# A cached-attention and MLP kernel for one token: K's first loads move to the head of the DMA stream, and two rows of wq share a load behind them

## The chip, the cores and the metric

The kernel runs on one core of a Trainium2 chip. The metric is device time in microseconds (us), the median of several runs. A profile of one more execution shows what each engine did. The engines are TensorE (PE in the profile; PEld for its weight loads), VectorE (DVE), ScalarE (ACT), GpSimd (POOL) and SyncE (SP). Loads from memory are issued by SyncE's and ScalarE's sequencers and carried out by sixteen DMA engines.

## What is computed

One token x of 1024 values is normalized and goes through two branches, whose results are added to x. Branch A is attention of 32 query heads over a cache of 4 key/value heads, of which the last 4096 positions are used. Branch B normalizes once more and applies a two-layer MLP. Cut to what matters, with B = Sq = 1, D = 1024, Hq = 32, Hkv = 4, Dh = 128, W = 4096, F = 3584, all in bf16:

```python
xn = layernorm(x)
q = (xn @ wq).reshape(1, 1, 32, 128)
k = repeat(k_cache[:, :, Sk - 4096:, :], 8, axis=1)
v = repeat(v_cache[:, :, Sk - 4096:, :], 8, axis=1)
o = softmax(q k^T * 128 ** -0.5) @ v
a = o.reshape(1, 1, 4096) @ wo
b = gelu(layernorm(xn) @ w1 + b1) @ w2 + b2
out = x + a + b
```

Nearly all bytes are read once: K and V 4 MB each, `wq` and `wo` 8 MB each, `w1` and `w2` 7 MB each.

## The kernel before

Four buffers of 4 MB (`slot[0]` to `slot[3]`, 128 partitions by 32 KB each) take all large loads in turn. `slot[0]` receives K, `slot[1]` and `slot[2]` receive `wq` rows 0 to 3 and 4 to 7 of each partition, and `slot[3]` is scratch for K's transposes. Later `w1`, V, `w2` and `wo` go into the same buffers as these come free.

Each of K's four head groups is one load (`load_k`, L193): 32 rows of 32 KB, each row going to one partition, group g to partitions g, g + 4, g + 8 and so on (L194). `wq` is seen as 128 partitions of eight rows of 8 KB (L190).

Six loads are issued ahead of everything else, at L199: by SyncE row 0 of `wq` and K's groups 0 to 3, and by ScalarE the small x (32 rows of 64 bytes). Then comes a barrier of all engines (L203), and after it the work that the class `Plan` (L15) writes out: the code lists operations with the names that each reads and writes, in the order in which each engine is to run them, and `Plan.emit` (L27) adds the waits between engines. Nothing is reordered. Lines 235 to 238 enter the early loads into this list without issuing them again, so that later operations can wait for their semaphores. Lines 244 to 246 issue the rest of `wq`: row 1, rows 2 and 3, rows 4 to 7.

SyncE's queue is served in the order of issue. After `wq` it issues the small `b1` and `b2` (L322, L323), the two halves of `w1` (L383, L384), V (L387), three parts of `w2` (L431, L432) and seven parts of `wo` (L506, L509), each once the buffer it overwrites is free. The line in the profile for all these is that of the helper that issues, L213.

What the other engines do around the change:

- GpSimd builds constants from L254 on, of which `spread` (L255) is needed by the first matmul.
- TensorE spreads x over the partitions (four small matmuls, L277), sums for the first LayerNorm, and then runs the product with `wq` in three pieces: a loop over rows 0 and 1 (L369), rows 2 and 3 (L370 to L377), and a loop over rows 4 to 7 (L378). Matmuls without a loop carry the helpers' lines L227 and L233, and weight loads L219.
- VectorE runs the LayerNorm's small operations (L280 to L313). Then it transposes K in four pieces of 128 x 4096 values (L334), each of which waits for all four groups of K. From L343 it copies ten of sixteen blocks of the result into `kT`; ScalarE copies the other six (L339). Scores, softmax, the product with V, and sums over 21 rows of `w2` (L482) follow.
- At the end TensorE takes `wo` rows as they land (L227). VectorE adds the bulk into `run[0]` (L550), the result is cast (L569, L570), and SyncE and ScalarE store one half each (L572, L573).

Of the kernel before, what the change touches and what calls it, by code (L numbers as in the profile page):

```python
# [132 lines left out]
def kernel(  # L133
# [14 lines left out]
    nc = tc.nc  # L148
    P = 128
    D = A_x.shape[-1]  # L150
    Hkv = A_k_cache.shape[1]
    Sk = A_k_cache.shape[2]
    Dh = A_k_cache.shape[3]
    NQ = A_wq.shape[1]
    Hq = NQ // Dh
    REP = Hq // Hkv
    Fd = B_w1.shape[1]
    W = min(4096, max(256, Sk // 4))
# [15 lines left out]
    def sb(name, shape, dt):  # L174
        return nc.alloc_sbuf_tensor(name, shape, dt).ap()

    def ps(name, shape):
        return nc.alloc_psum_tensor(name, shape, FP32).ap()

    slot = [sb(f"slot{i}", [P, 16384], BF16) for i in range(4)]  # L180
    kT = sb("kT", [P, 4, 4, W // 4], BF16)
    acc2 = ps("acc2", [P, 2, 512])
# [3 lines left out]

    x_flat = A_x.rearrange("a b d -> (a b d)")
    k_sb, kt_scr = slot[0], slot[3]
    k_sem = [nc.alloc_semaphore(f"k{g}") for g in range(Hkv)]
    wq_v = A_wq.rearrange("(p c) n -> p c n", p=P)  # L190
    wq_sem = nc.alloc_semaphore("wq0")

    def load_k(g):  # L193
        return nc.sync.dma_start(out=k_sb[g:P - Hkv + g + 1:Hkv, :],  # L194
                                 in_=A_k_cache[0, g, Sk - W:Sk, :].rearrange("(r c) d -> r (c d)", r=P // Hkv))

    x32 = sb("x32", [Hq, Hq], BF16)
    x_sem = nc.alloc_semaphore("x32")
    for i, sem in [(nc.sync.dma_start(out=slot[1][:, 0:NQ], in_=wq_v[:, 0, :]), wq_sem)] + [(load_k(g), k_sem[g]) for g in range(Hkv)] + [(nc.scalar.dma_start(out=x32, in_=x_flat.rearrange("(a j) -> a j", a=Hq)), x_sem)]:  # L199
        i.then_inc(sem, 16)  # L200
        tc.no_tile_sem_insts.add(i.ins.name)
    tc.close()
# [2 lines left out]
    plan = Plan(nc)  # L205
    pe, dve, act, pool, sp = nc.tensor, nc.vector, nc.scalar, nc.gpsimd, nc.sync

    def op(eng, fn, r=(), w=()):
        plan.add(eng, fn, r, w)
# [5 lines left out]
    def ldw(w_ap, pos, r):  # L215
        def go():
            with nc.discard():
                i = pe.ldweights(w_ap, tile_position=pos).ins
            return pe.add_instruction(mybir.InstLdweights(  # L219
                name=nc.get_next_instruction_name(), engine=i.engine, tile_size=(P, 32), tile_position=pos, ins=i.ins, outs=i.outs))  # L220
        op("pe", go, r, ())

    def mm(out_ap, w_ap, x_ap, start, stop, pos, r, w):
        def go():
            with nc.discard():
                i = pe.matmul(out_ap, lhsT=w_ap, rhs=x_ap, start=start, stop=stop, tile_position=pos).ins
            return pe.add_instruction(mybir.InstMatmult(  # L227
                name=nc.get_next_instruction_name(), engine=i.engine, start_tensor_calc=start, stop_tensor_calc=stop,
                tile_size=i.tile_size, tile_position=i.tile_position, ins=i.ins, outs=i.outs, ldweights=False))
        op("pe", go, r, w)  # L230

    def mm32(out_ap, w_ap, x_ap, start, stop, r, w, pos=None):
        op("pe", lambda: pe.matmul(out_ap, lhsT=w_ap, rhs=x_ap, start=start, stop=stop, tile_position=pos), r, w)  # L233

    plan.add("sp", lambda: None, (), ("wq0",), wq_sem)
    for g in range(Hkv):
        plan.add("sp", lambda: None, (), (f"k{g}",), k_sem[g])
    plan.add("act", lambda: None, (), ("x32",), x_sem)

    w1_v = B_w1.rearrange("(p c) n -> p c n", p=P)  # L240
    w2_v = B_w2.rearrange("(p c) n -> p c n", p=P)
    wo_v = A_wo.rearrange("(p c) n -> p c n", p=P)
    wq_t = [slot[1 + i].rearrange("p (r n) -> p r n", r=4) for i in range(2)]
    wq_cuts = ((0, 1, 2), (0, 2, 4), (1, 0, 4))
    for i, a, b in wq_cuts:
        dma("sp", wq_t[i][:, a:b, :], wq_v[:, 4 * i + a:4 * i + b, :], (), (f"wq{4 * i + a}",))

# [48 lines left out]
    xw = sb("xw", [P, 96 + C * P], BF16)  # L296
# [32 lines left out]
    scr = kt_scr.rearrange("p (s f) -> p s f", s=NS)  # L329
    k2 = k_sb.rearrange("p (s f) -> p s f", s=NS)  # L330
    T5 = kt_scr.rearrange("p (s c a j) -> p s c a j", s=NS, a=4, j=32)
    T3 = kt_scr.rearrange("p (c a j) -> p c a j", a=4, j=32)
    for s in range(NS):
        op("dve", lambda s=s: dve.transpose(out=scr[:, s, :], in_=k2[:, s, :]), ("k0", "k1", "k2", "k3", "slot0"), (f"scr{s}",))  # L334
    pairs = [(R, Cd) for R in range(4) for Cd in range(4)]
    ACT_PAIRS = 6
    for s0, s1 in ((0, 1), (1, 2), (2, 4)):
        for (R, Cd) in pairs[:ACT_PAIRS]:
            op("act", lambda s0=s0, s1=s1, R=R, Cd=Cd: act.copy(out=kT[32 * Cd:32 * Cd + 32, R, s0:s1, :].rearrange("p s (c j) -> p (s c) j", j=32),  # L339
                                                                in_=T3[32 * R:32 * R + 32, 32 * s0:32 * s1, Cd, :]), [f"scr{s}" for s in range(s0, s1)], (f"kTa{R}{Cd}{s0}",))  # L340
    kt_keys = [f"kTa{R}{Cd}{s}" for (R, Cd) in pairs[:ACT_PAIRS] for s in range(3)]
    for n, (R, Cd) in enumerate(pairs[ACT_PAIRS:]):
        op("dve", lambda R=R, Cd=Cd: dve.tensor_copy(out=kT[32 * Cd:32 * Cd + 32, R, :, :].rearrange("p s (c j) -> p (s c) j", j=32),  # L343
                                                     in_=T3[32 * R:32 * R + 32, :, Cd, :]), [f"scr{s}" for s in range(NS)], (f"kTd{R}{Cd}",))
# [8 lines left out]
    def pe_loop(name, steps, body):  # L353
        at = pe.alloc_register(f"{name}_at")
        pe.reg_mov(at, 0)
        pe.br(f"{name}_rows")
        only = [mybir.EngineType.PE]
        nc.enter_bb(f"{name}_rows", valid_engines=only)
        body(pe.snap(at, min_val=0, max_val=steps - 1))
        pe.reg_add(at, at, 1)  # L360
        pe.br_lt(at, steps, f"{name}_rows", f"{name}_done")
        nc.enter_bb(f"{name}_done", valid_engines=only)

    def wq_rows(i, per):
        def rows(at):
            for u in range(per):
                n = per * at + u
                for b in range(2):
                    pe.matmul(acc2[:, b, :], lhsT=xw[:, bass.ds(32 * n + 512 * i, P)],  # L369
                              rhs=slot[1 + i][:, bass.ds(1024 * n + 512 * b, 512)], start=False, stop=False)  # L370
        return rows

    qz, zrow = qm.rearrange("p g h -> p (g h)")[0:Hq, :], spread.rearrange("p u n -> p (u n)")
    for b in range(2):
        mm32(acc2[:, b, :], qz, zrow, True, False, ("qm", "spread"), ("acc2",))
    op("pe", lambda: pe_loop("wq0", 8, wq_rows(0, 1)), ("xw", "wq0", "wq1"), ("acc2",))
    for c in (2, 3):  # L377
        for t in range(4):  # L378
            ldw(xw[:, 96 + P * c:97 + P * c], (0, 32 * t), ("xw",))
        for b in range(2):  # L380
            for t in range(4):
                j = 2 * (3 - t) + b
                mm(acc2[32 * t:32 * t + 1, b, :], xw[:, 96 + P * c:97 + P * c], wq_t[0][:, c, j * 512:(j + 1) * 512],  # L383
                   False, False, (0, 32 * t), ("wq0", "wq1", "wq2", "slot1"), ("acc2",))  # L384
    op("pe", lambda: pe_loop("wq1", 8, wq_rows(1, 2)), ("xw", "wq4", "slot2"), ("acc2",))
    for b in range(2):
        mm32(acc2[:, b, :], qz, zrow, False, True, ("qm", "spread", "slot2"), ("acc2",))  # L387
# [21 lines left out]
    for b in range(2):  # L409
        for hh in range(4):  # L410
            k = 4 * b + hh
# [130 lines left out]
    def wo_row(c):  # L542
        i, r = divmod(c, 16)
        return wo_t[i][:, r, :], f"wo0{r // 8 * 8}" if i == 0 else f"wo1{max(a for a in cuts if a <= r)}"
# [9 lines left out]
    for c in range(NB, CWO):  # L554
        wap, key = wo_row(c)
# [49 lines left out]
```

## Time and profile before

| what | value |
|---|---|
| median of 3 runs | 100.47 us (100.42 to 100.51) |
| the profiled execution | 100.62 us, of which the span is 98.8 us |
| granted TensorE clock, mean | 0.896 |
| busy: TensorE / VectorE / ScalarE / GpSimd | 57.2 / 73.9 / 30.7 / 10.0 us |
| bytes read | 39.86 MB, 403 GB/s over the span |
| K, one group: time from issue to landing (median of four) | 9.8 us |
| x: time from issue to landing | 3.5 us |
| last wq load (4 MB): time from issue to landing | 27.0 us |

The span runs from the first to the last instruction of the execution that was profiled; the rest of its time lies before and after. The strip of slices shows the busy share of each engine in tenths, in 40 equal stretches of the span. In a line of the waits, the numbers are the idle time in total, how often it happened and the longest; in a line of the timeline or of the chain, the start and the duration. A line of the windows gives the stretch, its length, the busy time and number of instructions of PE, PEld, DVE, ACT and POOL, then the granted clock, the DMA share and GB/s, where a packet counts in the window in which it starts. The trace also records every packet of the DMA engines by itself: its start, its duration, its size and its queue, but not which of the sixteen engines carried it.

### The profile page before, as it was taken

Reading aid. Unit: us, or ns where it says so; the run is one execution under the profiler, and the core shown is the slowest. Engines: PE = TensorE matmul, PEld = TensorE weight load, DVE = VectorE, ACT = ScalarE, POOL = GpSimd, SP = SyncE. Lnnn points to the kernel's source line nnn. Section 1 sums busy time; section 2 is a strip of 40 time slices with the busy share of each in tenths; the row PEclk is TensorE's granted clock in tenths of the full one; section 3 lists DMA queues with packets and bytes.
Section 4 is the critical chain, followed back from the end, with each engine's and each line's share of the span. In section 5 each row is a group of like instructions: output and inputs, shape, how many; then the busy total and the mean of one; then the engine's idle time right before and its main releaser. Section 6 shows DMA issues by size and latency. Waiting matters only on the chain.

```text
span 98.8 us, 961 instructions
## 1 busy us (share of the span) xinstructions
PE 57.2 (58%) x323; PEld 16.2 (16%) x220; DVE 73.9 (75%) x75; ACT 30.7 (31%) x29; POOL 10.0 (10%) x22
## 2 busy tenths in 40 slices
PE   0032040598200699960899586667670999594792
PEld 0022000123000233410202121212210111110130
DVE  0023776999999999999102677899999999999431
ACT  0050000089999899992001075100000000000001
POOL 0072580000000680000000000000000000000000
PEclk9999999999985556997558999999999589999999
DMA  3999979999999999999799999999998999999970
GB/s 50 448 418 451 464 328 458 441 511 438 424 424 405 395 453 453 395 441 464 338 424 424 418 441 413 463 424 429 487 418 383 431 431 424 424 424 405 405 265 1
DMA packets 3132, 39.86 MB, mean 403 GB/s; under 512 B 438, under 2 KB 444, under 8 KB 828
## 3 DMA queue, kind: packets, MB, share of 16 engines
q1 hardware_dynamic: 3082, 39.86, 95.4%
q10 hardware_dynamic: 50, 0.00, 0.0%
HBM read 39.86 MB, written 0.00 MB: 403 GB/s over the span
## 4 chain that ended last, share of the span: by engine, by line
DVE 36%; DMA 32%; PE 20%; issue 5%; SPq 2%; ACT 2%; DVEq 0%
DMA slot<-in_A_wo_dram 20%; DVE slot L334 18%; DVE kT L343 13%; DMA slot<-in_A_k_cache_dram 13%; PE qo_ps L495 10%; PE sc_ps L227 6%; PE acc L227 2%; SPq L194 2%; ACT e L450 1%; DVE eTb L454 1%; DVE m_loc L435 1%; PE acc L233 1%; DVE q_sb L388 1%; ACT sc L427 1%; DVE res L569 0%
## 5 line engine op out<-in xcount | busy, mean ns | idle before, releaser
L339 ACT COPY kT<-slot 32x1024 bf16<-32x1024 bf16 (+1 forms) x18 | 23.9, 1327 | 14.3 <-DVE slot L334 14.1
L482 DVE SCALAR_TENSOR_TENSOR run<-slot,hTf,run 128x1024 f32<-128x1024 bf16 x20 | 24.2, 1272 | 0.0
L369 PE MATMUL acc<-slot,xw 128*128 x48 | 15.7, 494 | 12.6 <-DMA slot<-in_A_wq_dram 12.2
L334 DVE STREAM_TRANSPOSE slot<-slot 128x4096 bf16<-128x4096 bf16 x4 | 17.4, 4414 | 1.2 <-DMA slot<-in_A_k_cache_dram 1.2
L343 DVE COPY kT<-slot 32x4096 bf16<-32x4096 bf16 x10 | 13.2, 1316 | 0.2
L495 PE MATMUL qo_ps<-slot,eTb 128*128 (+1 forms) x32 | 10.2, 382 | 5.1 <-issue 4.0
L227 PE MATMUL sc_ps<-slot,o 128*1 128x512 bf16 x48 | 9.1, 378 | 2.8 <-DMA slot<-in_A_wo_dram 2.8
L369 PEld LDWEIGHTS acc<-slot,xw 128*128 x48 | 5.5, 115 | 23.5 <-issue 21.1
L570 ACT CAST res<-acc 33x224 bf16<-33x224 f32 x1 | 0.3, 338 | 20.1 <-PE acc L227 20.1
L227 PE MATMUL sc_ps<-kT,qm 128*32 128x512 bf16 x32 | 6.1, 973 | 0.3 <-DVE qm L416 0.3
L495 PEld LDWEIGHTS qo_ps<-slot,eTb 128*128 (+1 forms) x32 | 3.1, 96 | 12.0 <-issue 8.7
L428 DVE COPY sc<-sc_ps 128x512 f32<-128x512 f32 x1 | 0.7, 691 | 5.7 <-PE sc_ps L227 5.7
L227 PE MATMUL sc_ps<-slot,hT 128*1 128x512 bf16 x14 | 4.7, 509 | 0.1
L538 ACT CAST o<-misc 128x32 bf16<-128x32 f32 x1 | 0.2, 186 | 14.6 <-PE misc L233 14.6
L219 PEld LDWEIGHTS <-o 128*1 128x1 bf16 x40 | 2.4, 83 | 12.4 <-issue 11.8
L233 PE MATMUL misc<-x,spread 32*128 32x8 bf16 x4 | 0.3, 168 | 6.2 <-POOL spread L255 6.2
L249 DVE MEMSET mhalf<- 128x1 f32 x1 | 0.1, 59 | 5.0 <-PEq L203 5.0
L233 PE MATMUL acc<-spread,qm 32*128 32x512 bf16 x4 | 1.6, 498 | 3.7 <-POOL qm L315 3.7
L227 PE MATMUL acc<-slot,yT 128*1 128x448 bf16 x64 | 3.4, 353 | 0.0
L427 ACT COPY sc<-sc_ps 128x512 f32<-128x512 f32 x1 | 0.6, 585 | 8.8 <-PE sc_ps L227 8.8
L251 ACT ACT_TABLE_LOAD x1 | 1.3, 1283 | 4.8 <-PEq L203 4.8
L227 PE MATMUL acc<-slot,o 128*1 128x288 bf16 (+1 forms) x32 | 2.2, 272 | 0.6 <-DMA slot<-in_A_wo_dram 0.6
(88 smaller groups left out, 46.0 us busy)
## 6 DMA issues: line engine op xcount, KB each, us to landing
slot<-in_B_w_dram SPq DMA_DIRECT2D x3, 3584.0 KB, 16.6
slot<-in_A_wo_dram SPq DMA_DIRECT2D x3, 2048.0 KB, 22.8
slot<-in_A_k_cache_dram SPq DMA_DIRECT2D x4, 1024.0 KB, 9.8
slot<-in_A_wq_dram SPq DMA_DIRECT2D x1, 4096.0 KB, 27.0
slot<-in_A_v_cache_dram SPq DMA_DIRECT2D x1, 4096.0 KB, 16.1
slot<-in_A_wq_dram SPq DMA_DIRECT2D x2, 1024.0 KB, 9.2
slot<-in_A_wq_dram SPq DMA_DIRECT2D x1, 2048.0 KB, 17.8
slot<-in_B_w_dram SPq DMA_DIRECT2D x1, 2048.0 KB, 21.5
```

Source lines behind the costliest of these rows:

```text
L194: return nc.sync.dma_start(out=k_sb[g:P - Hkv + g + 1:Hkv, :], in_=A_k_cache[0, g, Sk - W:Sk, :].rearrange("(r c) d -> r (c d)", r=P // Hkv))
L219: return pe.add_instruction(mybir.InstLdweights(name=nc.get_next_instruction_name(), engine=i.engine, tile_size=(P, 32), tile_position=pos ...
L227: return pe.add_instruction(mybir.InstMatmult(name=nc.get_next_instruction_name(), engine=i.engine, start_tensor_calc=start, stop_tensor_c ...
L233: op("pe", lambda: pe.matmul(out_ap, lhsT=w_ap, rhs=x_ap, start=start, stop=stop, tile_position=pos), r, w)
L251: op("act", lambda: act.activation(out=dummy[:, 0:1], in_=mhalf[0:1, 0:1], func=ACT.Exp), ("mhalf",), ("act_warm",))
L334: op("dve", lambda s=s: dve.transpose(out=scr[:, s, :], in_=k2[:, s, :]), ("k0", "k1", "k2", "k3", "slot0"), (f"scr{s}",))
L339: op("act", lambda s0=s0, s1=s1, R=R, Cd=Cd: act.copy(out=kT[32 * Cd:32 * Cd + 32, R, s0:s1, :].rearrange("p s (c j) -> p (s c) j", j=32), ...
L343: op("dve", lambda R=R, Cd=Cd: dve.tensor_copy(out=kT[32 * Cd:32 * Cd + 32, R, :, :].rearrange("p s (c j) -> p (s c) j", j=32), in_=T3[32 ...
L369: pe.matmul(acc2[:, b, :], lhsT=xw[:, bass.ds(32 * n + 512 * i, P)], rhs=slot[1 + i][:, bass.ds(1024 * n + 512 * b, 512)], start=False, st ...
L427: op("act", lambda: act.copy(out=sc[:, 512:1024], in_=sc_ps[:, 1, :]), ("sc1",), ("scs1",))
L482: op("dve", lambda: dve.scalar_tensor_tensor(out=t, in0=wap, scalar=hTf[:, c:c + 1], in1=t, op0=ALU.mult, op1=ALU.add), (key, "hTf", f"run ...
L495: return pe.matmul(qo_ps, lhsT=cols, rhs=v4[:, :, c, :], start=first, stop=last)
```

## The change

K moves to the head of SyncE's stream. Its group 0 is split into two loads of sixteen rows, the even ones and the odd ones (partitions 0, 8, 16 and so on, and 4, 12, 20 and so on). Groups 1 to 3 stay loads of 32 rows. `wq` row 0 leaves the head, and one load issued after the barrier brings rows 0 and 1. The number of SyncE's loads is the same, five ahead of the barrier and three of `wq` behind it. The transposes wait for five semaphores of K instead of four, and the matmuls with `wq` rows 0 to 3 wait for one load less. Every other instruction keeps its place on its engine.

```diff
     k_sb, kt_scr = slot[0], slot[3]
-    k_sem = [nc.alloc_semaphore(f"k{g}") for g in range(Hkv)]
+    RK = P // Hkv
+    k_parts = [(0, 0, 2), (0, 1, 2)] + [(g, 0, 1) for g in range(1, Hkv)]
+    k_sem = [nc.alloc_semaphore(f"k{g}{b}") for g, b, _ in k_parts]
     wq_v = A_wq.rearrange("(p c) n -> p c n", p=P)
-    wq_sem = nc.alloc_semaphore("wq0")
-
-    def load_k(g):
-        return nc.sync.dma_start(out=k_sb[g:P - Hkv + g + 1:Hkv, :],
-                                 in_=A_k_cache[0, g, Sk - W:Sk, :].rearrange("(r c) d -> r (c d)", r=P // Hkv))
+
+    def load_k(g, b, step):
+        rows = A_k_cache[0, g, Sk - W:Sk, :].rearrange("(r c) d -> r (c d)", r=RK)
+        return nc.sync.dma_start(out=k_sb[g + Hkv * b:P - Hkv * (step - b) + g + 1:Hkv * step, :], in_=rows[b:RK - step + b + 1:step, :])
...
-    for i, sem in [(nc.sync.dma_start(out=slot[1][:, 0:NQ], in_=wq_v[:, 0, :]), wq_sem)] + [(load_k(g), k_sem[g]) for g in range(Hkv)] + [(nc.scalar.dma_start(out=x32, in_=x_flat.rearrange("(a j) -> a j", a=Hq)), x_sem)]:
+    for i, sem in [(load_k(*p), s) for p, s in zip(k_parts, k_sem)] + [(nc.scalar.dma_start(out=x32, in_=x_flat.rearrange("(a j) -> a j", a=Hq)), x_sem)]:
...
-    plan.add("sp", lambda: None, (), ("wq0",), wq_sem)
-    for g in range(Hkv):
-        plan.add("sp", lambda: None, (), (f"k{g}",), k_sem[g])
+    k_keys = tuple(f"k{g}{b}" for g, b, _ in k_parts)
+    for key, sem in zip(k_keys, k_sem):
+        plan.add("sp", lambda: None, (), (key,), sem)
...
-    wq_cuts = ((0, 1, 2), (0, 2, 4), (1, 0, 4))
+    wq_cuts = ((0, 0, 2), (0, 2, 4), (1, 0, 4))
...
-        op("dve", lambda s=s: dve.transpose(out=scr[:, s, :], in_=k2[:, s, :]), ("k0", "k1", "k2", "k3", "slot0"), (f"scr{s}",))
+        op("dve", lambda s=s: dve.transpose(out=scr[:, s, :], in_=k2[:, s, :]), k_keys + ("slot0",), (f"scr{s}",))
...
-    op("pe", lambda: pe_loop("wq0", 8, wq_rows(0, 1)), ("xw", "wq0", "wq1"), ("acc2",))
+    op("pe", lambda: pe_loop("wq0", 8, wq_rows(0, 1)), ("xw", "wq0"), ("acc2",))
...
-                   False, False, (0, 32 * t), ("wq0", "wq1", "wq2", "slot1"), ("acc2",))
+                   False, False, (0, 32 * t), ("wq0", "wq2", "slot1"), ("acc2",))
```

## Prediction

> **What bounds the kernel now.** I read the page's strip of slices and its queue table first, then the waits, the chain of waits, the order of SyncE's issues, and last the first microseconds cut into short windows.
>
> ```profile
> span 98.8 us, 961 instructions
> ...
> DMA  3999979999999999999799999999998999999970
> ...
> q1 hardware_dynamic: 3082, 39.86, 95.4%
> ```
>
> SyncE's queue (q1) carries 39.86 MB, and its packets fill 95.4% of sixteen DMA engines' time over the whole span. The strip shows no slice in which the engines stand still between the first and the last. The waits say the same at the end of the kernel:
>
> ```profile
> PE sc_ps L227 <- DMA slot<-in_A_wo_dram: 2.8, 3, 1.3
> ...
> DVE run L550 <- PE sc_ps L227: 1.5, 1, 1.5
> ...
> DVE slot L334 <- DMA slot<-in_A_k_cache_dram: 1.2, 1, 1.2
> ```
>
> TensorE waits for pieces of `wo` to land, VectorE's last sum (L550) waits 1.5 us for TensorE, and VectorE's first transpose of K (L334) waits 1.2 us for K. The third line is where K's arrival is felt. The chain of waits has K in it as well:
>
> ```profile
> 3.10 12.46 DMA slot<-in_A_k_cache_dram
> ...
> 15.58 17.44 DVE slot L334 x4
> ...
> 74.51 19.40 DMA slot<-in_A_wo_dram
> ```
>
> This chain must be read with care. The last line is a load of 1 MB that needed 19.40 us because it was queued behind loads issued earlier. A chain that issues it sooner does not make it land sooner, so the K part of the chain does not bound the end. To see how far it is from bounding, I compare each issue on SyncE with the landing of the load before it (issue time plus time to landing):
>
> ```profile
> 25.46 7.90 SPq L213 DMA_DIRECT2D slot<-in_B_w_dram  x2
> 43.57 0.38 SPq L213 DMA_DIRECT2D slot<-in_A_v_cache_dram  x1
> 46.35 9.38 SPq L213 DMA_DIRECT2D slot<-in_B_w_dram  x3
> 58.77 17.59 SPq L213 DMA_DIRECT2D slot<-in_A_wo_dram  x7
> ```
>
> The load issued at 25.46 stands behind the last `wq` load, which lands at 32.6 (issued 5.61, 27.0 us to landing). The `v` load issued at 43.57 stands behind a `w1` load issued at 33.04 that lands at 49.7 (16.6 us). The smallest margin is that one, 6.1 us. So every issue may move several microseconds either way and the engines still never run out of work. The end is the start of the stream, plus its bytes at the engines' pace, plus a short tail (last piece of `wo` landed at 96.5, last matmul over at 96.83, casts, store).
>
> **The change part by part.** The new order of SyncE's loads is K's group 0 as sixteen rows and sixteen rows, groups 1 to 3, then `wq` rows 0-1, 2-3, 4-7. It was eight loads and is eight loads, with the same bytes. TensorE, VectorE, ScalarE and GpSimd keep every instruction in its place.
>
> *K lands earlier.* It loses the 1 MB in front of it: eight packets of 8 KB on each engine, start to start 0.306 us by the trace's records of single packets, 2.45 us. It landed at 15.56, so now near 13.1. VectorE can't use all of that. Before L334 stand the LayerNorm operations (the last ends at 14.41), and these wait for x.
>
> *x lands later.* x goes through ScalarE's queue, and in the packet records its two rows and its semaphore each come after one packet of the other queue, so three packets pass first. Those were 8 KB (0.309 us); they become K rows of 32 KB (1.213 us each): 3 x 0.904 = 2.7 us later, 4.28 becomes about 7.0. TensorE's first matmul ran at 6.20, held by GpSimd's `spread`, so 1.9 us of this lies under GpSimd and 0.8 us is left. LayerNorm then ends at 15.2 and the transposes start at 15.2 instead of 15.58. Behind that VectorE is earlier by 0.4 us, with 1.5 us of idle before L550 as before. For the end this is worth 0.00. If x came later than that, VectorE would hold the end once LayerNorm ends 2.6 us late (1.18 us of idle before L334 and 1.46 before L550), which needs x at 8.8.
>
> *`wq` rows 0-1 as one load.* TensorE's first loop waited for both rows already. They end at the same place in the stream (6.3 MB in, landing 18.0), so its start stays. Packets of 16 KB take 0.613 us against 2 x 0.309; start to start that saves 2 ns, 8 packets per engine: -0.02 us. `wq` rows 0-1 stop being SyncE's two issues and become one, K's group 0 becomes two: no issue more or less.
>
> *One more cut in K.* Between two loads each engine handles one 4-byte semaphore packet of 9 ns; one is added in K and one goes from `wq`: 0.00. [...]
>
> *The head of the stream.* This is the part with a price. These windows give the DMA share and GB/s in the last two columns:
>
> ```profile
> 0.00:1.75 1.75, 0.00 (x0) 0.00 (x0) 0.00 (x0) 0.00 (x0) 0.20 (x4) 1.00 0.00 0
> 1.75:2.25 0.50, 0.00 (x0) 0.00 (x0) 0.00 (x0) 0.00 (x0) 0.00 (x0) 1.00 1.45 229
> 2.25:2.75 0.50, 0.00 (x0) 0.00 (x0) 0.00 (x0) 0.00 (x0) 0.00 (x0) 1.00 0.44 115
> 2.75:3.25 0.50, 0.00 (x0) 0.00 (x0) 0.00 (x0) 0.00 (x0) 0.00 (x0) 1.00 0.80 314
> 3.25:4.75 1.50, 0.00 (x0) 0.00 (x0) 0.00 (x0) 0.00 (x0) 0.00 (x0) 1.00 1.04 437
> ```
>
> The first load is issued at 0.80 and nothing moves until 1.81. Then for 1.5 us the mean is 219 GB/s, against 437 right after: 1.5 x (1 - 219/437) = 0.75 us of stream time lost. The packet records show how: the sixteen engines start one after another from 1.81 to 2.58 (mean 2.04), and most first packets take 0.55 to 1.24 us instead of 0.31. The first load has 128 rows, eight per engine. The new first load has sixteen rows, one per engine.
>
> The trace of before has no such load at the head, so I bound it. The nearest row for a load of few rows is the last store: issued at 97.38, its packet moves at 98.17, 0.79 us later, against 1.01 for the first of the 128-row load and 1.78 for its last engine. With 0.79 to 1.01 all engines start between 1.59 and 1.81, middle 1.70, which is 0.34 us before the present mean of 2.04. Best case: the whole loss of 0.75 us goes. Worst case: a K load takes longer to issue (0.53 to 0.61 us, against 0.40 for the `wq` load), which starts everything 0.13 to 0.21 us later with no gain. I take the middle value of 0.34, since one descriptor per engine is nearest to the store, and I leave the slowness of the first packets as it is.
>
> The sum: -0.34 - 0.02 = -0.36 us. The profiled execution had a span of 98.8 and 100.62 in all, so 1.8 us lies around the span; it becomes 98.4 and 100.26. The median of the runs is 0.15 us under the profiled one, so the forecast on the median is 100.47 - 0.36 = 100.11 us.
>
> **The rivals.**
>
> *The start is the same.* The 0.55 to 1.24 us of the first packets may be the memory's or the engines' own waking, whatever they are asked for. For it: engines that start late have short first packets, as if all waited for one moment. Against it: the spread from 1.81 to 2.58. Time: 100.47 - 0.02 = 100.45.
>
> *K issues slowly.* The four K issues of 0.53 to 0.61 us speak for it; that they stand behind other issues speaks against. Time: 100.58 to 100.66.
>
> *The first packet's slowness goes by bytes.* A mean first packet took 0.83 us for 8 KB, 2.7 times the normal one. If the factor holds for 32 KB, it takes 3.3 us, a loss of 2.1 us against 0.52 now: slower by 1.5, less the 0.34 of the earlier start, 101.7. It decides from a loss of 0.9 us in the first packet on. For it: the rate, not the count, is low in the windows. Against it: later packets show a fixed time per byte at once.
>
> *Sixteen rows share half the paths into memory (the slower side).* Even rows of group 0 go to partitions 0, 8, ... 120. If two engines then share one path, each row takes 2.43 us instead of 1.213, in both halves: 2 x 1.213 = +2.43, so 102.9. It decides as soon as a row of the first two loads takes over 1.4 us beyond its start-up. [...]
>
> **How the numbers follow.** Chances: forecast 0.50, same start 0.14, slow issue 0.08, by bytes 0.12, shared paths 0.16. The runs shown scatter by 0.09 us; 0.2% (0.20 us) is about what a measurement of this kernel can tell from no change. Faster: 0.47 of the forecast and 0.01 of the same start, 0.48. Same: 0.03, 0.11 and 0.04 of the slow issue, 0.18. Slower: the rest, 0.34. The likeliest case's own range is 99.7 (the whole 0.75 us) to 100.4. The range for 8 in 10 goes from 99.6 to 101.5, which takes in the slow issue and the lower half of the loss by bytes, and leaves out shared paths.
>
> **What would show it.** In the changed profile the first packets should move between 1.59 and 1.81, with over 219 GB/s in the 1.5 us from there; all later packets should keep 1.213 us per 32 KB. K should land near 12.8 to 13.1, x near 7, and the transposes start near 15.2. The last `wo` piece should land 0.36 us earlier, near 96.1. Rows of the first two loads at 2.4 us would make it shared paths, and a first packet over 3 us the loss by bytes. A DMA slice that empties in mid-span, or VectorE's L550 without idle time before it, would break the reading that only the stream's start counts.

## The result, and the profile after

The change made the kernel slower: 103.05 us (median of 5, 102.87 to 104.36) against 100.51 for the kernel before (median of 5, 100.42 to 100.67), a ratio of 1.0283 (95% interval 1.022 to 1.0346). The ratios leave out slow runs (over 1.5% above the fastest of the same kernel), carry a 95% interval, and need not equal the quotient of the medians. The forecast was 100.11 us. The spans of the five runs are 101.1 to 101.3 us against 98.8 before, so 2.4 us of the loss lie within the span. The profiled execution took 104.36 us, 3.2 us of it outside the span (1.8 before); what follows goes by the span.

The page of the changed kernel, from its span, its strip of slices and its queue table:

```profile
span 101.2 us, 960 instructions
...
DMA  4988979999999998998979999999989999999980
GB/s 117 259 246 376 453 317 421 440 434 460 414 427 427 457 453 374 476 419 385 521 321 421 421 427 432 445 434 411 521 363 427 421 447 414 421 414 418 405 311 1
...
q1 hardware_dynamic: 2954, 39.86, 95.2%
```

The share of the DMA engines' time is 95.2%, as good as before (95.4%). What they moved in it is not: the second to fourth slices stand at 259, 246 and 376 GB/s. A busy share says that packets were under way, not how fast. Cut into three stretches of 5 us, the windows of the kernel before and then of the kernel after (DMA share and GB/s are the last two columns):

```profile
1.75:6.75 5.00, 0.26 (x4) 0.18 (x4) 0.44 (x4) 1.49 (x2) 1.62 (x5) 1.00 1.10 420
6.75:11.75 5.00, 1.17 (x4) 1.00 (x4) 2.72 (x13) 0.00 (x0) 2.15 (x7) 1.00 0.97 419
11.75:16.75 5.00, 1.03 (x2) 0.13 (x2) 3.14 (x4) 0.00 (x0) 2.38 (x4) 1.00 0.93 395
```

```profile
1.75:6.75 5.00, 0.26 (x4) 0.18 (x4) 0.23 (x3) 1.49 (x2) 1.37 (x4) 1.00 0.96 223
6.75:11.75 5.00, 1.17 (x4) 1.00 (x4) 2.71 (x13) 0.00 (x0) 2.41 (x8) 1.00 1.02 406
11.75:16.75 5.00, 1.03 (x2) 0.13 (x2) 2.49 (x6) 0.00 (x0) 2.40 (x4) 1.00 0.94 403
```

In the first 5 us the stream moves 223 GB/s instead of 420: 5 x (1 - 223/420) = 2.35 us of stream time. The rest runs nearly as before. The trace's records of single packets show which packets are slow. Here are K's 32 KB packets in rounds of sixteen, in order of their start (durations in us, shortest to longest of the sixteen):

```
round                 1             2             3             4 to 8
kernel before    1.21 to 1.26  1.21 to 1.23  1.21 to 1.21  1.21
kernel after     1.71 to 2.45  2.29 to 2.37  1.45 to 2.26  1.21 to 1.23
```

Rounds 1 and 2 of the kernel after are the two loads of sixteen rows. Their rows take about 2.3 us, nearly twice 1.213, and the records of the next load are longer as well. The landings of the loads, told by their semaphores in the trace, are clearer: the two halves land at 6.05 and 8.37, and groups 1 to 3 at 10.68, 13.11 and 15.55, 2.31 to 2.44 us apart. Before, the four whole groups landed 2.43 to 2.45 us apart (8.25, 10.68, 13.13, 15.56); now the second half, with half the bytes, takes 2.32 us. By the landings the loss lies in the two halves alone.

The last packet of `wo` ends at 98.38 instead of 96.05, 2.33 us later, which is nearly the whole loss of the span. SyncE's store of the result follows it in step. Its line in the timeline before, then after:

```profile
97.38 0.27 SPq L213 DMA_DIRECT2D out_dram<-res  x1
```

```profile
99.75 0.27 SPq L214 DMA_DIRECT2D out_dram<-res  x1
```

K gained nothing. The first line is the DMA view's for K's two half loads, and the second the one for x; the last figure is the time from issue to landing:

```profile
slot<-in_A_k_cache_dram SPq DMA_DIRECT2D x2, 512.0 KB, 6.1
...
x<-in_A_x_dram ACTq DMA_DIRECT2D x1, 2.0 KB, 1.5
```

The half groups need 6.1 us (median of the two). VectorE's timeline then shows the transposes starting when they did before (15.58), though 1 MB less is in front of K:

```profile
13.04 0.73 DVE L314 TENSOR_REDUCE sel<-ident_f 128x32 f32<-128x128 f32 x1
15.57 4.45 DVE L335 STREAM_TRANSPOSE slot<-slot 128x4096 bf16<-128x4096 bf16 x1 [1.80 <-DMA slot<-in_A_k_cache_dram]
```

### The profile page after: what moved, and what is told of

It is laid out like the page before. It is cut to its first block, busy times and chain, and to the rows that moved or that the text cites. A ratio compares the mean times of both kernels' runs of the same rounds, so it can differ in the third digit from the quotient of the medians.

```text
span 101.2 us, 960 instructions
## 1 busy us (share of the span) xinstructions
PE 56.0 (55%) x323; PEld 16.2 (16%) x220; DVE 73.1 (72%) x75; ACT 30.8 (30%) x29; POOL 10.0 (10%) x22
## 3 DMA queue, kind: packets, MB, share of 16 engines
q1 hardware_dynamic: 2954, 39.86, 95.2%
## 4 chain that ended last, share of the span: by engine, by line
DMA 65%; PE 24%; issue 3%; SPq 1%; DVE 0%
DMA slot<-in_A_wq_dram 29%; DMA slot<-in_A_wo_dram 19%; DMA slot<-in_A_v_cache_dram 17%; PE qo_ps L496 11%; PE acc L370 9%; PE acc L228 2%; PE acc L234 1%; SPq L214 1%; DVE res L570 0%
## 5 line engine op out<-in xcount | busy, mean ns | idle before, releaser
L370 PE MATMUL acc<-slot,xw 128*128 x48 | 15.2, 488 | 14.4 <-DMA slot<-in_A_wq_dram 14.4
L496 PE MATMUL qo_ps<-slot,eTb 128*128 (+1 forms) x32 | 11.5, 458 | 8.1 <-DMA slot<-in_A_v_cache_dram 5.5
L228 PE MATMUL sc_ps<-kT,qm 128*32 128x512 bf16 x32 | 3.9, 638 | 0.3 <-DVE qm L417 0.3
L551 DVE TENSOR_TENSOR run<-sc_ps,run 33x512 f32<-33x512 f32 x2 | 1.3, 678 | 1.9 <-PE sc_ps L228 1.9
```

Source lines behind the costliest of these rows:

```text
L228: return pe.add_instruction(mybir.InstMatmult(name=nc.get_next_instruction_name(), engine=i.engine, start_tensor_calc=start, stop_tensor_c ...
L496: return pe.matmul(qo_ps, lhsT=cols, rhs=v4[:, :, c, :], start=first, stop=last)
L551: op("dve", lambda half=half: dve.tensor_tensor(out=run[0][0:33, 512 * half:512 * half + 512], in0=bulk[:, half, :], in1=run[0][0:33, 512 ...
```

## The experiments

Five theories stood at one time or another. A, shared paths: rows that go to certain partitions at the same time share a path into SBUF. B, the head: whatever comes first pays by bytes. C: a load with one row per engine is slow by itself. D: source rows 64 KB apart are slow. E came later: a crowded path holds up all engines. Paths are a conjecture: the runs record what packets take and when loads land, not the way a row goes.

### Undoing the split (e1)

```diff
-    k_parts = [(0, 0, 2), (0, 1, 2)] + [(g, 0, 1) for g in range(1, Hkv)]
+    k_parts = [(g, 0, 1) for g in range(Hkv)]
```

> K stays at the head and wq rows 0-1 stay one load, but K's group 0 is one load of 32 rows again. Theory A (shared paths: the sixteen rows of one load go to partitions 8 apart, so two engines share one path into SBUF): no K packet over 1.4 us but the first of each engine, end of stream 2.3 us before the changed kernel's, 100.1 to 100.7 us. Theory B (the head: whatever comes first pays until about 8 us, by bytes): the first three 32 KB packets of each engine stay at 2.2, 2.3 and 1.7 us, 102.5 to 103.1. Theory C (one row per engine in a load is slow) and theory D (source rows 64 KB apart in memory are slow) expect what A expects.

Measured: 100.83 us against 100.50, ratio 1.004 (1.0015 to 1.0065). Its windows over the same stretches:

```profile
1.75:6.75 5.00, 0.53 (x6) 0.45 (x6) 0.55 (x4) 1.49 (x2) 1.87 (x7) 1.00 1.07 420
6.75:11.75 5.00, 0.91 (x4) 0.74 (x4) 2.77 (x13) 0.00 (x0) 2.08 (x5) 1.00 0.97 419
```

420 GB/s is back, with K still at the head. The first packets take 1.25 to 2.08 us (start-up included) and all later ones 1.21 to 1.30, and the stream ends at 96.08, 2.30 us before the changed kernel's. So the split costs these 2.3 us. B is out for the second and third rounds.

The move itself gains nothing. The stream of this one trace ends within 0.03 us of the kernel before, but that pair flatters it: the ten runs of e1 have spans of 98.9 to 99.2 us (median 99.0), and those of the kernel before on the same chip 98.5 to 98.9 (median 98.65). The 0.33 us between the medians of the times lies within the span.

e1 also tests what the forecast built on. VectorE's timeline and waits in e1:

```profile
12.36 1.62 DVE L314 TENSOR_REDUCE sel<-ident_f 128x32 f32<-128x128 f32 x1
13.14 4.45 DVE L335 STREAM_TRANSPOSE slot<-slot 128x4096 bf16<-128x4096 bf16 x1
```

```profile
DVE run L551 <- PE sc_ps L228: 1.9, 1, 1.9
```

K's transposes start 2.44 us earlier than before, and the end does not come earlier. The last sum's idle time grows from 1.5 to 1.9 us. K's arrival was not what bounded the kernel.

### Moving the split (e2), and another way to split (e3)

e2 puts `wq` row 0 back at the head and row 1 behind K, and keeps the two half loads (not shown: the semaphore of row 0 and the waits for rows 0 and 1, which are those of the kernel before):

```diff
...
-    for i, sem in [(load_k(*p), s) for p, s in zip(k_parts, k_sem)] + [...]:
+    for i, sem in [(nc.sync.dma_start(out=slot[1][:, 0:NQ], in_=wq_v[:, 0, :]), wq_sem)] + [(load_k(*p), s) for p, s in zip(k_parts, k_sem)] + [...]:
...
-    wq_cuts = ((0, 0, 2), (0, 2, 4), (1, 0, 4))
+    wq_cuts = ((0, 1, 2), (0, 2, 4), (1, 0, 4))
...
```

> The order of the kernel before (wq row 0 at the head, row 1 behind K) with K's group 0 split into even and odd rows. Theories A, C and D: the 32 packets of the split group take about 2.3 us each wherever they stand in the stream, 102.5 to 103.0 us. Theory B: K rows behind 1 MB of wq take 1.21 us, 100.4 to 100.8 us.

Measured: 103.80 us, ratio 1.029 (1.0217 to 1.0364), above A's 102.5 to 103.0. The stream ends at 98.41, 2.36 us after the kernel before, as A has it; the four spans are 101.2 to 101.7 us, and up to 3.2 us of a time lie outside them. The windows show the loss where the half loads now stand:

```profile
1.75:6.75 5.00, 0.00 (x0) 0.00 (x0) 0.22 (x2) 1.32 (x2) 1.10 (x2) 1.00 1.04 322
6.75:11.75 5.00, 1.44 (x8) 1.18 (x8) 2.34 (x11) 0.17 (x1) 2.67 (x10) 1.00 1.03 308
11.75:16.75 5.00, 1.03 (x2) 0.12 (x2) 2.58 (x8) 0.00 (x0) 2.38 (x4) 1.00 0.98 419
```

The packets of the two rounds take 1.86 to 2.30 and 2.36 to 2.37 us. The loss goes with the split, not with the place; B is out altogether.

e3 splits group 0 into rows 0-15 and 16-31:

```diff
-        return nc.sync.dma_start(out=k_sb[g + Hkv * b:P - Hkv * (step - b) + g + 1:Hkv * step, :], in_=rows[b:RK - step + b + 1:step, :])
+        n = RK // step
+        return nc.sync.dma_start(out=k_sb[g + Hkv * n * b:g + Hkv * (n * (b + 1) - 1) + 1:Hkv, :], in_=rows[n * b:n * (b + 1), :])
```

> The changed kernel with group 0 split into rows 0-15 and 16-31, so that source rows are 32 KB apart and partitions 4 apart (0 to 60, then 64 to 124). [...] Theory D (source rows 64 KB apart): 1.21 us per row, 100.1 to 100.7 us.

Measured: 103.05 us, ratio 1.0198 (1.0126 to 1.027). There is a loss; whether it is over 2% the interval leaves open. The packets of the second round take 2.34 to 2.36 us (one of them 3.15), and the stream ends at 98.16. The source rows are side by side in memory here, so D is out.

### 32 rows in partitions side by side (e4)

e1, with the partitions of its loads changed:

```diff
-        return nc.sync.dma_start(out=k_sb[g + Hkv * b:P - Hkv * (step - b) + g + 1:Hkv * step, :], in_=rows[b:RK - step + b + 1:step, :])
+        return nc.sync.dma_start(out=k_sb[RK * g:RK * (g + 1), :], in_=rows[b:RK - step + b + 1:step, :])
```

> As e1, but each group of K goes to 32 partitions side by side (group 0 to 0-31, group 1 to 32-63 and so on); K's rows then lie in other partitions than the later work takes them from, and only the time is of use. All loads have 32 rows, two per engine, source rows 32 KB apart. [...] Theories B, C and D: 1.21 us per packet, the time of e1.

Measured: 110.81 us (two runs), ratio 1.1013 (1.0935 to 1.109). The windows:

```profile
1.75:6.75 5.00, 0.00 (x0) 0.00 (x0) 0.22 (x2) 1.49 (x2) 2.24 (x9) 1.00 1.14 249
6.75:11.75 5.00, 1.42 (x8) 1.19 (x8) 1.13 (x8) 0.00 (x0) 0.00 (x0) 1.00 0.98 203
11.75:16.75 5.00, 1.03 (x2) 0.13 (x2) 2.90 (x10) 0.00 (x0) 3.65 (x6) 1.00 1.01 210
```

About half the rate (203 GB/s in the second window, where e1 has 419), for as long as K's loads last: after the first round all packets take 2.39 to 2.57 us, against 1.21 to 1.30 in e1. Source, size and number of rows are e1's, and only the partitions differ. That the set of partitions alone can halve the rate is shown here, for loads of 32 rows.

### The same cut, by columns (e11)

```diff
-        return nc.sync.dma_start(out=k_sb[g + Hkv * b:P - Hkv * (step - b) + g + 1:Hkv * step, :], in_=rows[b:RK - step + b + 1:step, :])
+        n = 16384 // step
+        return nc.sync.dma_start(out=k_sb[g:P - Hkv + g + 1:Hkv, n * b:n * (b + 1)], in_=rows[:, n * b:n * (b + 1)])
```

> The changed kernel with K's group 0 cut by columns: two loads of 32 rows of 16 KB each, in place of two loads of sixteen rows of 32 KB. The same bytes, the same number of loads, the same place. Theory A: 32 rows at a step of four partitions share no path; packets of 16 KB at 0.61 us, 100.4 to 100.9 us. If two loads of 0.5 MB at the head cost by being small: as the changed kernel, 102.9 to 103.1 us.

Measured: 101.84 us (100.98 to 101.95), ratio 1.0101 (1.0045 to 1.0156), above what A expected and below the changed kernel. The half loads themselves are not slow: after the first packet of each engine, all take 0.608 to 0.652 us, and both have landed by 5.93 (8.37 in the changed kernel). So two loads of 0.5 MB are not slow by being small. The loss comes behind them, where the stream ends at 97.26. From 5.58 to 6.35 only 14 packets are in flight, and four of the first rows of group 1 take 1.9 to 2.35 us. My guess is that rows of engines that fell behind meet those of others; no run shows it.

### One extra load, three sets of partitions (e5, e6, e7)

These are e1 with one more load of sixteen rows into the scratch buffer. Between them only its partitions differ (the line of step 8):

```diff
+        if step == 2:
+            return nc.sync.dma_start(out=kt_scr[0:121:8, :], in_=rows[0:RK - 1:2, :])
```

> e1 with one extra load of 0.5 MB behind K's group 0: the sixteen even rows of group 0 once more, into partitions 0, 8, ... 120 of the scratch buffer. By its bytes alone it costs 1.21 us. Theory A (shared paths): two rows per path, all sixteen packets about 2.3 us, so 2.3 to 2.8 us over e1. Theory C (one row per engine is slow) and theory D (source rows 64 KB apart are slow): the same.

> The same extra load, the same rows of memory, but into partitions 0, 7, ... 105. [...] Theories C and D: all sixteen 2.3 us, as with step 8.

> The same extra load into partitions 0 to 15. [...] Theories C and D: 2.3 us per packet, as with step 8.

Measured: 103.23, 103.25 and 106.13 us (two runs each; ratios 1.0261, 1.0262 and 1.0548). The windows of the extra load, for step 8, step 7 and step 1 in turn:

```profile
5.10:8.10 3.00, 0.85 (x6) 0.68 (x6) 0.89 (x6) 1.33 (x2) 2.08 (x9) 1.00 1.19 350
```

```profile
5.10:8.10 3.00, 0.85 (x6) 0.68 (x6) 0.90 (x6) 1.33 (x2) 2.07 (x9) 1.00 1.14 350
```

```profile
5.10:8.10 3.00, 0.85 (x6) 0.68 (x6) 0.94 (x7) 1.22 (x2) 1.96 (x9) 1.00 1.23 175
```

Step 8 costs what A says (2.3 to 2.8 us): the stream ends at 98.60, 2.52 us after e1's 96.08, and the extra load lands 2.29 us after group 0 (8.46 and 6.17), though its sixteen records show 1.69 to 2.08 us. Step 1 is worse than the 2.3 us per packet of theories C and D: its packets take 2.98 to 4.15 us and the stream ends at 101.02. That is 4.94 us after e1's end; the extra bytes explain 1.21, and 3.73 us are left, about three more turns of 1.21. Theories C and D by themselves have no room for that. At step 7 the sixteen packets take 1.54 to 1.90 us, the load lands 2.31 us after group 0 (8.39 and 6.08), and the stream ends at 98.50, 2.52 us before that of step 1. The loss is that of step 8.

### Eight rows (e9, e10)

The same extra load with rows 0 to 7 of group 0, to partitions 0 to 28 (`kt_scr[0:29:4, :]`) and 64 to 92 (`kt_scr[64:93:4, :]`).

> e1 with one extra load of eight rows (0.25 MB) behind K's group 0, into partitions 0, 4, ... 28 of the scratch buffer, one row on each of eight engines. [...] Theory C (a load with one row per engine is slow by itself): eight packets at 2.3 us, end 2.3 us after e1's.

> The same eight rows into partitions 64, 68, ... 92. [...] Theory C: eight packets at 2.3 us and all K rows at 1.21, as in the other variant.

Measured: 102.67 and 102.86 us (two runs each; ratios 1.0208 and 1.0227). In e9 seven of the eight extra packets take 1.22 us, and all land by 7.13, 1.23 us after group 0 (5.90): with eight rows, one row per engine is not slow by itself, so C is out for eight rows. In e10 they land up to 0.6 us later (7.33 to 7.77). But in both variants rows of K's group 1 take up to 2.4 us, and the streams end 2.0 and 1.7 us after e1's (98.07 and 97.76). What slows those rows is not shown; this stayed open.

### The same partitions four times in a row (m8, m7, m3)

To see the pace without the neighbours, the extra load became four of 8 KB rows, one column quarter after the other, at steps of 8, 7 and 3 partitions (the line of step 7):

```diff
+        if step == 2:
+            return nc.sync.dma_start(out=kt_scr[0:106:7, 4096 * b:4096 * b + 4096], in_=rows[0:RK // 2, 4096 * b:4096 * b + 4096])
```

> e1 with four extra loads of sixteen rows of 8 KB each behind K's group 0 (four column quarters of the scratch buffer, the same sixteen partitions 0, 8, ... 120 each time, source rows 32 KB apart), so that each engine writes the same partition four times in a row. An 8 KB packet took 0.309 us in the kernel before. [...]

> The same with partitions 0, 7, ... 105. [...] Theory C: all 64 at 0.62. Theory E (a crowded path holds up all engines, which the extra load at step 7 before suggests): all 64 between 0.4 and 0.5 us.

> The same with partitions 0, 3, ... 45. [...] Theory C: all 64 at 0.62. [...]

Measured, as the durations of sixteen packets in order of start (us; an 8 KB packet took 0.309 in the kernel before):

```
round      1              2              3              4
step 8     0.31 to 0.45   0.31 to 0.54   0.40 to 0.63   0.62 to 0.65
step 7     0.31           0.31 to 0.52   0.53 to 0.62   0.54 to 0.62
step 3     0.31 to 0.31   0.31 to 0.92   0.90 to 1.07   1.06 to 1.07
```

The times of these single runs were 103.34, 103.48 and 105.04 us. Two things are to be seen. The first packets show 0.31 us and the pace shows later, but the landings have it from the start: group 0 and the first two extra loads land at 6.29, 6.91 and 7.52 for step 7, and at 6.40, 7.53 and 8.59 for step 3. So the loads land 0.61 to 0.62 us apart at step 7 and 1.06 to 1.13 at step 3, where the first records show 0.31. That a record ends before its packet is written is a reading. It fits the changed kernel, where records of the round behind the half loads are long (1.45 to 2.26 us) and group 1 lands on time, 2.31 us after the second half. And in the fourth round all sixteen packets go at about one pace, 2.0 times 0.309 us for steps 8 and 7 and 3.4 times for step 3.

Theory E has the right form, one pace for all, and the wrong size for step 7 (landings 0.61 to 0.62 us apart instead of 0.4 to 0.5). Whether a crowded path is behind that pace was not tried.

A rival stays open here. Theory C had forecast 0.62 us for step 7, and that is what came, at step 8 as well. It fails by itself at step 3 (1.06 to 1.07) and step 1, and for eight rows in e9; but a load of exactly sixteen rows might go at half speed whatever its partitions, and slower still with some sets of them. In no run did a load of sixteen K rows go at full pace; one that did would tell the two apart.

### A second queue at the head (e8)

The kernel before, with K's group 0 issued by ScalarE behind x (not shown: the list of early loads at L199, which now puts x ahead of K):

```diff
-        return nc.sync.dma_start(out=k_sb[g:P - Hkv + g + 1:Hkv, :],
+        return (nc.scalar if g == 0 else nc.sync).dma_start(out=k_sb[g:P - Hkv + g + 1:Hkv, :],
...
```

> The kernel before with K's group 0 issued by ScalarE behind x, so that SyncE's wq row 0 and a K load with 32 rows are at the engines at the same time. If the 0.75 us lost at the head comes from engines that have only one queue's packet to work on while it starts up, a second queue fills it: up to 0.5 us less, 100.0 us. If the loss lies in the engines or the memory, no change: 100.5 us.

Measured: 100.49 us, ratio 1.000 (0.997 to 1.0029). The stream ends at 95.82 instead of 96.05, too little to tell in the time. No version beat the kernel before.

## Why the prediction was wrong

*What bounds the kernel.* Right. In every profiled run the span ends 2.7 to 2.9 us after the stream, and e1 advanced K by 2.44 us for nothing.

*K lands earlier.* Right for the move: e1 lands K at 13.12, forecast near 13.1. In the changed kernel the split ate it: 15.55. The step behind it was wrong: "VectorE can't use all of that", because the LayerNorm's last record ends at 14.41. In e1 the transposes start at 13.14, right at K's landing, while the record of the operation before them (L314) runs from 12.36 to 13.98. Such a record's end was not when VectorE became free, so VectorE may have had more room before L334 than the 1.18 us of the prediction.

*x lands later.* Wrong. x's packets went first (1.80 to 1.99), before K's first at 2.20, and x landed at 2.33 instead of 4.28; I had expected 7.0. A K load needs 0.61 us on SyncE's queue and x 0.39 on ScalarE's, so x reached the engines earlier. In e4, where the first K load needed 0.40 us to issue, x did wait behind K rows and took 7.9 us to land. For the end x made no difference.

*`wq` rows 0-1 as one load, and one more cut.* No run tries either alone, and nothing in the runs speaks against 0.02 and 0.00 us as prices by themselves. e1, which has the one and not the other, is 0.33 us slower than the kernel before by the medians and 0.35 by the spans; which of its parts costs that stays open.

*The head of the stream.* This is the step that failed: "I take the middle value of 0.34", a gain of 0.34 us, where the end of the stream came 2.33 us later. Two mistakes lie in it. The smaller one is the start, which was not earlier: the first packet moved at 2.20, not between 1.59 and 1.81. Of the 0.39 us against 1.81, 0.21 are the longer issue of a load with a partition step (0.61 us where `wq` took 0.40), which I had priced as the worst case from the right rows; the rest lies between the issue's end and the first packet (0.78 us against 0.61) and is not explained. e1 starts late too, at 2.14, and its first 2 MB have landed at 8.29 against 8.25 before, so the gain of 0.34 did not come. The larger one is the rows. The sum put their change at nothing and priced them at 1.213 us, as K's rows had cost in loads of 32 rows; in the two loads of sixteen they took about 2.3, and that is the 2.30 us by which the changed kernel's stream ends after e1's. e4 shows that this price depends on the set of partitions that a load writes (2.39 to 2.57 us, against 1.21 to 1.30 in e1). The trace of before had no load of sixteen such rows, so the value had to be bounded from above by the 2.43 us of the rival, and the price of the head was a range from -0.75 to +2.43, not to +0.21.

*The rivals.* "Sixteen rows share half the paths" gave 102.9 and 0.16 of the chance; 103.05 came. It had the place, the rows and the size, and the range left it out. That two engines share a path was my assumption, and no run shows it; what the runs show is rows of about 2.3 us in the loads of sixteen, and that the set of partitions alone can bring 32-row loads to 2.39 to 2.57 (e4). That all K packets of before took 1.213 us was no evidence against this rival, as those loads had twice as many rows, in other sets of partitions. "By bytes" (101.7) fell with e2; its 0.83 us leaves out the engine that started last, and with it the mean is 0.80. "K issues slowly" was true of the issue. Its delay does not show at the end of e1's trace, but it may be part of the 0.33 us that e1 loses.

## What to carry to other kernels

Look at the set of partitions that one load writes before cutting it: half the rows can take as long as the whole load. Here both halves ran at about half speed (2.3 us a row instead of 1.21), at the head and behind `wq` alike. Price a row from a load with the same partitions, or take a range that reaches to twice the price; sixteen rows in partitions side by side cost four times as much here (e7: 4.94 us, where the bytes explain 1.21). And where the DMA engines are busy from end to end, read GB/s beside the busy share, for 0.96 of busy time was 223 GB/s here and 1.10 was 420.

## What the runs showed that I had not expected

- All sixteen packets of a round settle at about one pace (m3: 1.06 to 1.07 us in the fourth round; m7: 0.54 to 0.62). That one crowded path sets it is a reading, not shown.
- A load of 16 or 32 rows that step over partitions took 0.53 to 0.62 us to issue in the kernel before, the changed one and e1; with partitions side by side (e4) the first three took 0.39 to 0.41.
- A slow load was followed by long records in the load behind it (K's third round in the changed kernel, 1.45 to 2.26 us), while that load landed on time (2.31 us after the one before). Landings were the better measure of a load here.
- Rows of 32-row loads that otherwise take 1.21 us took up to 2.35 us behind the two column loads (e11). Why is not shown.
